# One fp32 product per head, two heads side by side in TensorE's rows, in place of three fp32r products of split operands

## The chip, the cores and the metric

The kernel runs on one core of one Trainium2 chip. The metric is the device time of one execution in microseconds, the median of three runs. The profile is of one execution of its own.

## The reference

Three layers follow one another: a linear recurrence over 768 steps for 4 batches of 8 heads of 48 channels, and two mixture layers (384 to 768 to 384 and 384 to 2048 to 384) on the 3072 tokens of 384 channels that it gives.

```python
for t in range(S):
    cur = np.einsum('bhd,bhe->bhde', u[None] * kt, vt)
    y[:, :, t] = np.einsum('bhd,bhde->bhe', rt, state + cur)
    state = wt[:, :, :, None] * state + np.einsum('bhd,bhe->bhde', kt, vt)
...
h = np.maximum(np.maximum(x @ w1, x @ w2), x @ w3)
return (h @ w_out).astype(np.float32)
...
h = x @ w_in
g = h - np.tanh(h)
return (g @ w_out).astype(np.float32)
```

## The kernel before, in words

**The recurrence** is done in 24 chunks of 128 steps, 6 to a batch; only the state goes from chunk to chunk. Partitions 0 to 47 and 64 to 111 hold the channels of the two heads of a pair, and the free axis the 4 pairs. For a chunk, `scans` takes running products of the decays w forwards (`fwd`) and backwards (`suf`) on VectorE, `decays` multiplies k by `suf` and r by `fwd` in place, `scores` makes k'r of every pair of steps on TensorE, `masked` copies the scores to `P` (ScalarE) and clears what lies in the future (GpSimd), `diagonal` writes the term with u (VectorE), `outputs` multiplies `P` by v and adds r times the state, and `outputs_out` copies the result out of PSUM and sends it by DMA into `xs`, the input of the first mixture layer. `key_turn` transposes k in 32 x 32 blocks on VectorE and sends the blocks through DRAM to their places, `key_order` copies them to `kcn`, and `state_mm`, `state_add` and `state_decay` carry the state on.

**Scores.** Chunks 0 to 4 (`c < EARLY`) multiply plain fp32: 8 products a chunk, each with 48 rows, head 0 in the array's rows 0 to 63 and head 1 in rows 64 to 127, into two banks (line 307). From chunk 5 on, `splits` (lines 284 to 292) first makes of k and of r a rounded fp32r part and the exact rest, r with zeros where the other head's rows are: per chunk three copies on ScalarE (287, 291 twice) and three subtractions on VectorE (288, 292 twice). `scores` then does three fp32r products (`mm3`, lines 491 to 493) of 128 x 256 for each pair, 12 a chunk, half of them in step `k0` and half in `k1`. From chunk 6 on `outputs_two` gives the output in two halves of two pairs, in steps `k3` and `k4`, into two banks: two products with the state of 112 columns (359), then four with v of 48 columns (362).

**The order of the work.** Chunks 0 to 3 come first (the prologue). Then six groups of 512 tokens go through the first mixture layer: 18 slots of 9 products with `WAh`, `WAl` (lines 491 to 493 on `xh`, `xl`), and after them 54 products with `WOh`, `WOl` (the O part). Beside the slots of group g the four chunks of group g+1 are worked on, five steps (`k0` to `k4`) each, spread over the slots; group 5 has none. Group 0 also converts weights from float64 (lines 64 to 73, 487, 488), 16 units of the 24. A scheduler puts the instructions of each engine into one fixed order, and each engine works its own through in that order. Line 683 splits the last part of the hidden layer (`hl`) of a group on VectorE; 410 and 411 split `xs` for the next group.

**Buffers.** `wt`, `rk` and `nt` hold a chunk's inputs. There are two of each, and a third (`third`) for chunk 2 alone, closed when the splits' pool opens; `load_next` loads two chunks ahead from chunk 3 on, all on SyncE's queue.

The banks in the rows are numbered from 85 on: `bank_89` to `bank_92` are `bank[4]` to `bank[7]`, that is the two score banks, `yab` and `dsb`; `rk_119` and `rk_120` are `rk[0]` and `rk[1]`, `P_127` and `P_128` the two `Pt`, `AS_130` and `AS_131` the two `ASt`.

Of the kernel before, what the change touches and what calls it, by code (L numbers as in the profile page):

```python
# [15 lines left out]
ALU = mybir.AluOpType  # L16
# [43 lines left out]

# float64 words (low, high) -> float32: sign and top exponent bit, 7 exponent bits and 23 of the mantissa;
# sizes below float32's are set to zero, those above to its largest
def abs_f64(act, raw, out):
# [26 lines left out]
def main_path(ctx, tc, wT, rkT, w0, rk0, nat, vpad, uT, ub, wA, wo1, wi2, wo2, outT, count):  # L90
# [11 lines left out]
    p_third = ExitStack()  # L102
    p_spl = ExitStack()
    wo1p = ctx.enter_context(pool_("wo1p"))
# [57 lines left out]

    Yb, spl = [], []

# [9 lines left out]
    def ring(c):  # L174
        return c if c < 3 else (c - 1) % 2

    def load_next(c):
        n = 3 if c == 0 else 4 if c == 1 else c + 2
        if c != 2 and n < NCH:
            load_att(n)  # L180

# [14 lines left out]

# [1 line left out]
    def aend():  # L198
# [53 lines left out]
    def key_turn(c):  # L252
        # blocks of 32 x 32 on the vector engine, the blocks' places through DRAM
        if needs_state(c):
            kb = fwd[:, 0:NP * C]
            dve.transpose(kb.rearrange("p (c a q) -> p c a q", c=4, q=32),
                          rk[ring(c)][:, 1].rearrange("p a (c q) -> p c a q", c=4))
            sp.dma_start(kbd[c % 2].rearrange("p a b q -> p (a b q)"), kb)
            src = kbd[c % 2].rearrange("(a i) c b q -> c i a (b q)", a=4)
            for q in range(4):  # L260
                sp.dma_start(kb[32 * q:32 * q + 32].rearrange("i (a x) -> i a x", a=4), src[q])
# [11 lines left out]

    # k a rounded part and the exact rest; r likewise, a head's columns zero in the other head's rows
    def splits_open():
        p_third.close()
        sp_ = p_spl.enter_context(pool_("spl"))
        spl.extend(sp_.tile([P, NP, C], F32R, name=f"k{x}") for x in "hl")
        spl.extend(sp_.tile([P, NP, 2, C], F32R, name=f"r{x}") for x in "hl")
        for t in spl[2:]:  # L280
            for j in range(2):
                act.mul(t[64 * j:64 * j + 64, :, 1 - j], ident[64 * j:64 * j + 64, None, :].to_broadcast([64, NP, C]), 0.0)

    def splits(c):
        r = rk[ring(c)]
        kh, kl, rh, rl = spl
        act.copy(kh, r[:, 1])
        dve.tensor_tensor(kl, r[:, 1], kh, ALU.subtract)
        for j in range(2):
            rows = slice(64 * j, 64 * j + 64)  # L290
            act.copy(rh[rows, :, j], r[rows, 0])
            dve.tensor_tensor(rl[rows, :, j], r[rows, 0], rh[rows, :, j], ALU.subtract)

    def scores(c, half, st):
        if c >= EARLY:
            st[half] = scb()
            kh, kl, rh, rl = spl
            for p in (2 * half, 2 * half + 1):
                mm3(st[half][:, p % 2 * 2 * C:(p % 2 + 1) * 2 * C], kh[:, p], kl[:, p],
                    rh[:, p].rearrange("p s t -> p (s t)"), rl[:, p].rearrange("p s t -> p (s t)"), True, True)  # L300
            return
        if half == 0:
            st["s"] = [scb(), scb()]
        for p in (2 * half, 2 * half + 1):
            for j in range(2):
                rows = slice(64 * j, 64 * j + HD)
                pe.matmul(st["s"][j][:, p * C:(p + 1) * C], rk[ring(c)][rows, 1, p, :], rk[ring(c)][rows, 0, p, :],
                          start=True, stop=True)

    def diagonal(c):  # L310
        for j, q in enumerate(probs(c)):
            d = sdt[c % 2][:, NP * j:NP * (j + 1), None] if c >= EARLY else sdt[c % 2][:, j::2, None]
            dve.copy_predicated(q, dmask[:, None, :].to_broadcast([P, NP, C]), d.to_broadcast([P, NP, C]))  # L313

# [4 lines left out]

    def masked(c, st, which=range(2)):  # L320
        for j in which:
            q = probs(c)[j]
            act.copy(q.rearrange("p a t -> p (a t)"), st[j] if c >= EARLY else st["s"][j])  # L323
            pool.affine_select(out=q, in_=q, compare_op=ALU.is_gt, fill=0.0, base=0,  # L324
                               pattern=[[0, NP], [1, C]], channel_multiplier=-1)
# [25 lines left out]

    def outputs_two(c, half, st):
        V, q = vals(c), probs(c)[half]
        first = c % NC_B == 0
        obk = (yab, st[1])
        to = slice(half * C, (half + 1) * C)
        if not first:
            for i in range(2):
                pe.matmul(obk[i][0:AC, to], ASt[c % 2][:, 2 * half + i], rk[ring(c)][:, 0, 2 * half + i], start=True, stop=False)  # L359
        for i in range(2):  # L360
            for j in range(2):
                pe.matmul(obk[i][64 * j:64 * j + HD, to], V[:, 2 * half + i, j], q[:, 2 * i + j], start=first, stop=True)  # L362

    def outputs(c, half, st=None):
        if c >= EARLY_B:
            return outputs_two(c, half, st)
        b = c % 2
        V = vals(c)
        Pc = probs(c)
        first = c % NC_B == 0  # L370
        for p in (2 * half, 2 * half + 1):
            if c < EARLY:
# [6 lines left out]
                pe.matmul(o, W[:, p, 0:2 * HD], Pc[0][:, p, :], start=False, stop=True)  # L379
                continue  # L380
            if not first:
                pe.matmul(yab[0:AC, p * C:(p + 1) * C], ASt[b][:, p], rk[ring(c)][:, 0, p, :], start=True, stop=False)
            for j in range(2):
                o = yab[64 * j:64 * j + HD, p * C:(p + 1) * C]
                h = 2 * p + j
                pe.matmul(o, nt[ring(c)][:, DM + h * HD:DM + (h + 1) * HD], ident, start=first, stop=False)
                pe.matmul(o, V[:, p, j], Pc[half][:, 2 * (p % 2) + j], start=False, stop=True)

    def outputs_out(c, col, st=None):
        if c < EARLY:  # L390
# [5 lines left out]
        y = yst[c % 2]  # L396
        if c >= EARLY_B:
            for i, o in enumerate((yab, st[1])):
                act.copy(y[0:AC, i::2], o[0:AC, 0:2 * C].rearrange("p (a t) -> p a t", a=2))
        else:  # L400
            act.copy(y[0:AC].rearrange("p a t -> p (a t)"), yab[0:AC])
        to = xs[:, :, col:col + C]
# [15 lines left out]
    def att_steps(c, col):  # L418
# [3 lines left out]
        def k0():  # L422
            scores(c, 0, st)
            if c >= EARLY:
                masked(c, st, [0])
            if n and n < EARLY_B:
                bonus(n)
            if n:
                scans(n)

        def k1():
            scores(c, 1, st)
            masked(c, st, [1] if c >= EARLY else [0, 1])
            if c < EARLY:
# [3 lines left out]
            if n:  # L438
                decays(n)
                if n == EARLY:  # L440
                    splits_open()
                if n >= EARLY:
                    splits(n)
                if n >= EARLY_B:
                    bonus(n)
                squares(n)
# [10 lines left out]
        def k3():  # L457
            outputs(c, 0, st)
            if n:
                bonus_sum(n)  # L460

        def k4():
            outputs(c, 1, st)
            outputs_out(c, col, st)
            if n and n < EARLY_B:
# [5 lines left out]
    def in_range():  # L471
        # every product of decays within 2^-60 .. 2^60: the chunk-wise form keeps float32's accuracy
        dve.tensor_scalar(sq, sq, 1.0, None, ALU.is_lt)
# [3 lines left out]

# [1 line left out]
    def w1_upto(n):  # L479
# [14 lines left out]

# [1 line left out]
    def pads(i):  # L496
# [6 lines left out]
    def warm(n):  # L503
        # columns for the array's activity monitor while it would rest
        for _ in range(n):
# [52 lines left out]
    for c in range(GROUPS[0]):  # L558
        st = {}
        n = c + 1  # L560
        scores(c, 0, st)
        scores(c, 1, st)
        key_turn_pe(c)
# [7 lines left out]
        state_decay(n)  # L571
        outputs(c, 0)
        outputs(c, 1)
        warm(WARM[3] if c < 2 else 0)
# [13 lines left out]

# [1 line left out]
    WO2 = W2a = None  # L590
# [43 lines left out]
    for g, gn in enumerate(GROUPS):  # L634
# [5 lines left out]
        if g == len(GROUPS) - 2:  # L640
            def w2_open():
                nonlocal W2a
                in_range()
                p_att.close()
                p_spl.close()
                yb = ctx.enter_context(pool_("yb", "right"))
# [59 lines left out]

# [1 line left out]
    hb = Ring([bank[0], bank[1]])  # L708
# [45 lines left out]

# [1 line left out]
@with_exitstack  # L756
# [115 lines left out]
def _layout(r, k, v, w, u, moe_w1, moe_w2, moe_w3, moe_w_out, moe2_w_in, moe2_w_out):  # L872
# [17 lines left out]

    # x: of tile k, rows 0..95 are the head pair k, rows 96..127 a third of the last pair
    row = np.arange(P)
# [51 lines left out]
```

## Time and profile before

| | |
|---|---|
| median of 3 runs | 907.84 us (907.41 to 911.14) |
| profiled execution, span | 906.0 us |
| TensorE busy (products) | 854.7 us, 94% |
| VectorE busy | 573.0 us, 63% |
| ScalarE busy | 373.0 us, 41% |
| GpSimd busy | 218.9 us, 24% |
| group 0 of the first layer | 55.4 to 133.6 us, its O part to 148.1 |
| group 5, without chunks beside it | 436.5 to 474.5 us |
| second layer alone | about 487 to 906 us |

The profile gives no time of its own around the span; the median lies 1.8 us above the span. Busy shares are means over stages with different limits, so the stages are read one by one. An fp32 product of the program shows as two records in the trace, an fp32r product as one.

### The profile page before, as it was taken

The page shows a single profiled execution, that of the slowest core. Times are in us where ns is not written, and L with a number is a line of the kernel's source. Part 1 is how long each engine was busy: PE and PEld are TensorE (multiplying, and loading weights), DVE is VectorE, ACT ScalarE, POOL GpSimd, SP SyncE. Part 2 cuts the span into 40 slices and gives each one's busy share as a digit, 9 for nine tenths or more (in the row PEclk, how much of TensorE's full clock was granted, in tenths as well). Part 3 has the DMA queues.
Part 4 walks back from the last instruction along what each step waited for, and adds up shares of the span by engine and source line. Part 5 has one row for each costly group of instructions (what it writes and reads, how often), then busy time and mean ns, then how long its engine had stood idle before and what let it go on. Part 6 is the DMA issues. An engine that isn't in the chain of part 4 may idle for free.

```text
span 906.0 us, 11870 instructions
## 1 busy us (share of the span) xinstructions
PE 854.7 (94%) x4342; PEld 678.0 (75%) x4342; DVE 573.0 (63%) x880; ACT 373.0 (41%) x736; POOL 218.9 (24%) x214
## 2 busy tenths in 40 slices
PE   7888789989989999999998999999999999999996
PEld 5767567868767877877886678888888888888884
DVE  8999998886766777785899944334334334333332
ACT  4655445445334454553446533223323224223232
POOL 6756443452433343351035300000000000000000
PEclk8989889999999999999999999999999999999999
DMA  8533533344134133332553300000000000000001
GB/s 258 174 123 97 172 85 102 109 118 130 54 104 131 48 116 114 102 108 68 156 152 106 87 1 6 31 0 22 14 1 35 1 1 35 0 1 35 1 0 39
DMA packets 40561, 66.47 MB, mean 73 GB/s; under 512 B 6256, under 2 KB 21360, under 8 KB 40496
## 3 DMA queue, kind: packets, MB, share of 16 engines
q1 hardware_dynamic: 40496, 65.64, 24.3%
q8 instruction: 36, 0.59, 0.3%
q14 instruction: 29, 0.24, 0.1%
HBM read 53.23 MB, written 8.65 MB: 68 GB/s over the span
## 4 chain that ended last, share of the span: by engine, by line
PE 55%; DVE 3%; DMA 1%; issue 1%; ACT 1%; POOL 0%; ACTq 0%; SPq 0%; DVEq 0%
PE bank L493 18%; PE bank L491 18%; PE bank L492 18%; DVE cv L73 1%; DVE cv L72 1%; DMA xs<-in_wi 0%; PE bank L362 0%; DMA xs<-in_wo 0%; DVE cv L71 0%; PE bank L359 0%; DVE hl L724 0%; DVE fwd L206 0%; DVE P L313 0%; DVE cv L70 0%; DVE rk L213 0%
## 5 line engine op out<-in xcount | busy, mean ns | idle before, releaser
L722 DVE TENSOR_TENSOR tmp<-bank,tmp 128x512 f32<-128x512 f32 x96 | 66.3, 691 | 174.8 <-ACT tmp L721 174.8
L491 PE MATMUL bank<-xh,WAh 128*128 128x512 f32 x324 | 136.2, 420 | 0.0
L721 ACT ACTIVATE tmp<-bank 128x512 f32<-128x512 f32 x96 | 57.4, 598 | 182.9 <-PE bank L493 182.9
L493 PE MATMUL bank<-xl,WAh 128*128 128x512 f32 x324 | 131.7, 406 | 0.0
L492 PE MATMUL bank<-xh,WAl 128*128 128x512 f32 x324 | 130.8, 404 | 0.0
L491 PE MATMUL bank<-hh,WO2h 128*128 128x512 f32 x288 | 114.1, 396 | 1.7 <-ACT hh L723 1.7
L493 PE MATMUL bank<-hl,WO2h 128*128 128x512 f32 x288 | 114.3, 397 | 0.7 <-DVE hl L724 0.7
L492 PE MATMUL bank<-hh,WO2l 128*128 128x512 f32 x288 | 113.7, 395 | 0.0
L724 DVE TENSOR_TENSOR hl<-tmp,hh 128x512 fp32r<-128x512 f32 x96 | 66.5, 692 | 59.1 <-PE bank L493 46.7
L723 ACT CAST hh<-tmp 128x512 fp32r<-128x512 f32 x96 | 59.5, 620 | 72.8 <-DVE tmp L722 72.7
L491 PEld LDWEIGHTS bank<-xh,WAh 128*128 128x128 f32 x324 | 62.5, 193 | 18.3 <-issue 5.8
L493 PEld LDWEIGHTS bank<-xl,WAh 128*128 128x128 f32 x324 | 62.6, 193 | 15.8 <-DVE xl L416 0.7
L492 PEld LDWEIGHTS bank<-xh,WAl 128*128 128x128 f32 x324 | 63.2, 195 | 11.9
L493 PEld LDWEIGHTS bank<-hl,WO2h 128*128 128x128 f32 x288 | 54.1, 188 | 16.0 <-DVE hl L724 3.3
L491 PEld LDWEIGHTS bank<-hh,WO2h 128*128 128x128 f32 x288 | 54.1, 188 | 15.6 <-ACT hh L723 3.2
L683 POOL TENSOR_TENSOR hl<-tmp,hh 128x512 fp32r<-128x512 f32 x30 | 44.1, 1471 | 87.3 <-ACT hh L682 87.2
L492 PEld LDWEIGHTS bank<-hh,WO2l 128*128 128x128 f32 x288 | 54.1, 188 | 12.8
L680 DVE TENSOR_TENSOR tmp<-bank,tmp 128x512 f32<-128x512 f32 x72 | 49.2, 684 | 15.1 <-PE bank L493 12.9
L313 DVE COPY_PREDICATED P<-dmask,sd 128x512 f32<-128x512 uint8 x36 | 35.7, 1011 | 25.2 <-POOL P L324 25.2
L324 POOL TENSOR_SCALAR_AFFINE_SELECT P<-P 128x512 f32<-128x512 f32 x44 | 33.2, 761 | 69.1 <-ACT P L323 69.0
L491 PE MATMUL bank<-xh,W2ha 128*128 128x512 f32 x108 | 43.5, 402 | 2.8 <-ACT Yb L704 2.8
L493 PE MATMUL bank<-hl,WOh 128*128 128x512 f32 x108 | 43.2, 402 | 2.9 <-DVE hl L683 1.6
(196 smaller groups left out, 1736.0 us busy)
## 6 DMA issues: line engine op xcount, KB each, us to landing
nt<-in_nat SPq DMA_DIRECT2D x19, 576.0 KB, 4.3
rk<-in_rkT SPq DMA_DIRECT2D x44, 192.0 KB, 3.3
Y<-in_wA SPq DMA_DIRECT2D x18, 384.0 KB, 5.5
w2st<-in_wi SPq DMA_DIRECT2D x12, 384.0 KB, 3.2
wt<-in_wT SPq DMA_DIRECT2D x44, 96.9 KB, 2.9
kbd<-fwd SPq DMA_DIRECT2D x15, 256.0 KB, 2.0
fwd<-kbd SPq DMA_DIRECT2D x60, 64.0 KB, 2.0
xs<-in_wo SPq DMA_DIRECT2D x8, 384.0 KB, 3.2
```

Of the source, the lines that this page charges most:

```text
L72: dve.scalar_tensor_tensor(oi, high, -0x40000000, oi, ALU.bitwise_and, ALU.bitwise_or)
L313: dve.copy_predicated(q, dmask[:, None, :].to_broadcast([P, NP, C]), d.to_broadcast([P, NP, C]))
L324: pool.affine_select(out=q, in_=q, compare_op=ALU.is_gt, fill=0.0, base=0, pattern=[[0, NP], [1, C]], channel_multiplier=-1)
L491: pe.matmul(bk, wh, ah, start=first, stop=False)
L492: pe.matmul(bk, wl, ah, start=False, stop=False)
L493: pe.matmul(bk, wh, al, start=False, stop=last)
L680: dve.tensor_tensor(t[:, 0:n], bk[:, 0:n], t[:, 0:n], ALU.max)
L683: (dve if f == F1 - 1 else pool).tensor_tensor(hl[:, f, 0:n], t[:, 0:n], hh[:, f, 0:n], ALU.subtract)
L721: act.activation(t, bk, AF.Tanh)
L722: dve.tensor_tensor(t, bk, t, ALU.subtract)
L723: act.copy(hh[:, r], t)
L724: dve.tensor_tensor(hl[:, r], t, hh[:, r], ALU.subtract)
```

## The change

All chunks take the plain fp32 scores of chunks 0 to 4, in one run in step `k0`, and `splits` with its pool goes. `outputs` runs once a chunk, in step `k4`, all four pairs into one bank; the product with the state is split into one of 48 columns for each head, so that the two heads of a pair stand in the two column halves in every term. The third buffer stays open and joins the ring, so inputs load three chunks ahead. Comments are taken out.

```diff
     def ring(c):
-        return c if c < 3 else (c - 1) % 2
+        return c % 3
     def load_next(c):
-        n = 3 if c == 0 else 4 if c == 1 else c + 2
-        if c != 2 and n < NCH:
-            load_att(n)
+        if c + 3 < NCH:
+            load_att(c + 3)
...
-    def splits_open():
...
-    def splits(c):
...
-    def outputs_two(c, half, st):
...
+    def scores(c, st):
+        st["s"] = [scb(), scb()]
+        for p in range(NP):
             for j in range(2):
                 rows = slice(64 * j, 64 * j + HD)
                 pe.matmul(st["s"][j][:, p * C:(p + 1) * C], rk[ring(c)][rows, 1, p, :], rk[ring(c)][rows, 0, p, :],
...
+    def outputs(c):
...
+            terms = []
             if not first:
-                pe.matmul(yab[0:AC, p * C:(p + 1) * C], ASt[b][:, p], rk[ring(c)][:, 0, p, :], start=True, stop=False)
+                terms.append(lambda j: (ASt[b][:, p, 64 * j:64 * j + HD], rk[ring(c)][:, 0, p, :]))
+            if c < EARLY_B:
+                terms.append(lambda j: (nt[ring(c)][:, DM + (2 * p + j) * HD:DM + (2 * p + j + 1) * HD], ident))
+            terms.append(lambda j: (V[:, p, j], Pc[j][:, p, :]))
+            for i, t in enumerate(terms):
+                for j in range(2):
+                    pe.matmul(yab[64 * j:64 * j + HD, p * C:(p + 1) * C], *t(j), start=i == 0, stop=i == len(terms) - 1)
...
         def k0():
-            scores(c, 0, st)
-            if c >= EARLY:
-                masked(c, st, [0])
+            scores(c, st)
+            masked(c, st)
...
         def k1():
-            scores(c, 1, st)
-            masked(c, st, [1] if c >= EARLY else [0, 1])
...
-                if n == EARLY:
-                    splits_open()
-                if n >= EARLY:
-                    splits(n)
...
         def k3():
-            outputs(c, 0, st)
             if n:
                 bonus_sum(n)
         def k4():
-            outputs(c, 1, st)
-            outputs_out(c, col, st)
+            outputs(c)
+            outputs_out(c, col)
```

In the rows that follow lines are those of each program: 491 to 493 before are 439 to 441 after, 307 is 278, 680 is 626, 683 is 629, 411 is 367, 313 is 283, 204 is 202 or 204 by its output, 212 and 213 are 210 and 211, 256 is 254.

TensorE, chunk 9's scores beside group 1's slots, before: six products, a slot of nine, six more.

```order
L491 MATMUL bank_89<-rh,kh 128x256
L492 MATMUL bank_89<-rh,kl 128x256
L493 MATMUL bank_89<-rl,kh 128x256
L491 MATMUL bank_89<-rh,kh 128x256
L492 MATMUL bank_89<-rh,kl 128x256
L493 MATMUL bank_89<-rl,kh 128x256
L491 MATMUL bank_87<-xh,WAh 128x512
```

The same place after, and the next product:

```order
L278 MATMUL bank_89<-rk_119 128x128
L278 MATMUL bank_90<-rk_119 128x128
L278 MATMUL bank_89<-rk_119 128x128
L278 MATMUL bank_90<-rk_119 128x128
L278 MATMUL bank_89<-rk_119 128x128
L278 MATMUL bank_90<-rk_119 128x128
L278 MATMUL bank_89<-rk_119 128x128
L278 MATMUL bank_90<-rk_119 128x128
L439 MATMUL bank_87<-xh,WAh 128x512
```

Twelve products in two places became eight in one, the banks of the two heads in turn.

VectorE at the end of group 0, before, from the last maximum of the hidden layer on:

```order
L680 TENSOR_TENSOR tmp_116<-bank_86,tmp_116 128x512
L205 RECIPROCAL d_126<-suf 128x4
L206 SCALAR_TENSOR_TENSOR fwd<-wt_118,d_126 128x516
L203 MEMSET d_126 128x5
L683 TENSOR_TENSOR hl<-tmp_116,hh 128x512
L212 TENSOR_TENSOR rk_120<-rk_120,suf 128x512
L213 TENSOR_TENSOR rk_120<-rk_120,fwd 128x512
L256 STREAM_TRANSPOSE fwd<-rk_120 128x512
L288 TENSOR_TENSOR kl<-rk_120,kh 128x512
L292 TENSOR_TENSOR rl<-rk_120,rh 64x4x128 x2
L232 TENSOR_REDUCE sd_135<-nt_122 128x8
L411 TENSOR_TENSOR xl<-xs,xh 128x512 x3
```

The same place after:

```order
L626 TENSOR_TENSOR tmp_116<-bank_86,tmp_116 128x512
L201 MEMSET d_126 128x5
L254 STREAM_TRANSPOSE fwd<-third 128x512
L629 TENSOR_TENSOR hl<-tmp_116,hh 128x512
L202 SCALAR_TENSOR_TENSOR suf<-wt_117,d_126 128x517
L203 RECIPROCAL d_126<-suf 128x4
L210 TENSOR_TENSOR rk_119<-rk_119,suf 128x512
L230 TENSOR_REDUCE sd_136<-nt_121 128x8
L367 TENSOR_TENSOR xl<-xs,xh 128x512
L283 COPY_PREDICATED P_127<-dmask,sd_135 128x512
L204 SCALAR_TENSOR_TENSOR fwd<-wt_117,d_126 128x516
L367 TENSOR_TENSOR xl<-xs,xh 128x512 x2
```

The scan of chunk 8 and its decays now stand ahead of `hl`, its three split operations are gone, and two of the three parts of `xl` stand behind a copy into `P` that needs chunk 8's scores and behind a scan of chunk 9.

## Rows read from the trace of the kernel before

**Rows 1.** Windows: us busy (instructions) of PE, PEld, DVE, ACT, POOL; clock, DMA.

```profile
55.40:133.60 78.20, 65.25 (x373) 50.25 (x372) 77.16 (x121) 39.77 (x86) 40.38 (x36) 0.89 0.36 111
...
148.10:208.20 60.10, 57.62 (x355) 45.50 (x353) 50.10 (x66) 26.86 (x58) 27.76 (x27) 0.97 0.38 112
...
221.10:281.10 60.00, 57.41 (x364) 44.77 (x362) 40.85 (x59) 25.43 (x54) 23.93 (x26) 0.97 0.32 92
281.10:295.80 14.70, 13.23 (x56) 10.10 (x55) 10.72 (x13) 6.97 (x15) 5.71 (x5) 1.00 0.42 125
...
351.90:366.20 14.30, 13.04 (x57) 10.20 (x55) 11.47 (x19) 7.30 (x17) 4.49 (x5) 1.00 0.48 140
...
436.50:474.50 38.00, 38.00 (x163) 30.52 (x163) 34.85 (x73) 18.35 (x36) 9.28 (x5) 1.00 0.50 143
```

**Rows 2.** Groups by form, TensorE, 148.1 to 423.7 us (groups 1 to 4).

```profile
L493 PE MATMUL bank<-rl,kh 128*128 128x256 f32 x64 | 18.9, 298 | 2.6 <-DVE rl L292 2.6
L491 PE MATMUL bank<-rh,kh 128*128 128x256 f32 x64 | 18.7, 292 | 1.9 <-ACT rh L291 1.6 <-ACT yst L399 0.2
L492 PE MATMUL bank<-rh,kl 128*128 128x256 f32 x64 | 18.6, 292 | 2.5 <-DVE kl L288 2.5
```

**Rows 3.** Timeline of TensorE in group 0: start, length, [idle before, what ended it].

```profile
118.57 0.58 PE L493 MATMUL bank<-rl,kh 128*128 128x256 f32 x1 [1.74 <-DVE rl L292]
```

**Rows 4.** Groups by form, VectorE, 55.4 to 133.6 us (group 0).

```profile
L292 DVE TENSOR_TENSOR rl<-rk,rh 64x512 fp32r<-64x512 f32 x6 | 6.0, 1008 | 0.1
L313 DVE COPY_PREDICATED P<-dmask,sd 128x512 f32<-128x512 uint8 x4 | 4.8, 1259 | 0.0
L206 DVE TENSOR_TENSOR_SCAN fwd<-wt,d 128x516 f32<-128x516 f32 x3 | 4.5, 1494 | 0.0
L212 DVE TENSOR_TENSOR rk<-rk,suf 128x512 f32<-128x512 f32 x3 | 3.9, 1284 | 0.0
...
L288 DVE TENSOR_TENSOR kl<-rk,kh 128x512 fp32r<-128x512 f32 x3 | 3.7, 1217 | 0.0
...
L213 DVE TENSOR_TENSOR rk<-rk,fwd 128x512 f32<-128x512 f32 x2 | 2.2, 1086 | 0.0
...
L256 DVE STREAM_TRANSPOSE fwd<-rk 128x512 f32<-128x512 f32 x2 | 1.4, 704 | 0.0
```

**Rows 5.** Line 288 over the whole span: ns least/median/most.

```profile
L288 DVE TENSOR_TENSOR kl<-rk,kh x19: 650/1110/1492, 75.7 to 403.0; 128x512 fp32r<-128x512 f32 x19
```

**Rows 6.** Timeline of TensorE in group 1: one half of a chunk's scores, and the next slot.

```profile
166.01 0.28 PE L491 MATMUL bank<-rh,kh 128*128 128x256 f32 x1
...
166.73 0.39 PE L491 MATMUL bank<-xh,WAh 128*128 128x512 f32 x1
```

**Rows 7.** Timeline of TensorE in the prologue: chunk 3's fp32 scores, and what follows.

```profile
40.81 1.18 PE L307 MATMUL bank<-rk 48*128 48x128 f32 x16
41.92 1.11 PE L271 MATMUL bank<-ident,rk 128*128 128x128 f32 x4
```

**Rows 8.** Timeline of TensorE in group 1: one half of a chunk's outputs, and the next slot.

```profile
203.80 0.60 PE L359 MATMUL bank<-rk,AS 128*112 128x128 f32 x4
204.33 0.64 PE L362 MATMUL bank<-P,nt 128*48 128x128 f32 x8
204.91 0.50 PE L491 MATMUL bank<-xh,WAh 128*128 128x512 f32 x1
205.24 0.40 PE L492 MATMUL bank<-xh,WAl 128*128 128x512 f32 x1
```

**Rows 9.** Timeline of TensorE, group 0's O part: the product that waits for `hl`.

```profile
139.36 0.51 PE L493 MATMUL bank<-hl,WOh 128*128 128x512 f32 x1 [1.29 <-DVE hl L683]
```

**Rows 10.** Windows of group 0 and the prologue, columns as in rows 1.

```profile
9.30:10.50 1.20, 1.09 (x16) 0.97 (x16) 1.17 (x2) 0.02 (x1) 1.20 (x2) 1.00 1.12 364
...
101.20:106.70 5.50, 5.00 (x25) 3.51 (x25) 5.50 (x7) 3.06 (x8) 3.98 (x4) 0.50 0.46 120
...
118.60:123.70 5.10, 5.10 (x15) 4.23 (x16) 5.10 (x10) 1.91 (x4) 1.72 (x2) 0.50 0.29 88
```

More of the change, by code (lines that the diff above doesn't have):

```diff
@@ L102, in main_path @@
     p_third = ExitStack()
-    p_spl = ExitStack()
     wo1p = ctx.enter_context(pool_("wo1p"))
@@ L161, in main_path @@
     kbd = [dramp.tile([P, 4, NP, 32], F32, name=f"kbd{i}") for i in range(2)]
-    Yb, spl = [], []
+    Yb = []
     def ys(d, g):
@@ L272, in key_turn_pe @@
             act.copy(kcn.rearrange("t b r -> t (b r)"), dsb)
-    def splits_open():
[L276 to L282, printed above, removed]
-    def splits(c):
[L285 to L294, printed above, removed]
-        if c >= EARLY:
[L296 to L304, printed above, removed]
+    def scores(c, st):
+        st["s"] = [scb(), scb()]
+        for p in range(NP):
             for j in range(2):
@@ L311, in diagonal @@
         for j, q in enumerate(probs(c)):
-            d = sdt[c % 2][:, NP * j:NP * (j + 1), None] if c >= EARLY else sdt[c % 2][:, j::2, None]
-            dve.copy_predicated(q, dmask[:, None, :].to_broadcast([P, NP, C]), d.to_broadcast([P, NP, C]))
+            dve.copy_predicated(q, dmask[:, None, :].to_broadcast([P, NP, C]),
+                                sdt[c % 2][:, j::2, None].to_broadcast([P, NP, C]))
     def bonus_vals(c):
@@ L318, in bonus_vals, with masked @@
             sdt[c % 2].rearrange("p (a s) -> p a s", s=2)[:, :, :, None].to_broadcast([P, NP, 2, HD]), ALU.mult)
-    def masked(c, st, which=range(2)):
-        for j in which:
+    def masked(c, st):
+        for j in range(2):
             q = probs(c)[j]
-            act.copy(q.rearrange("p a t -> p (a t)"), st[j] if c >= EARLY else st["s"][j])
+            act.copy(q.rearrange("p a t -> p (a t)"), st["s"][j])
             pool.affine_select(out=q, in_=q, compare_op=ALU.is_gt, fill=0.0, base=0,
@@ L350, in state_add @@
                     dve.tensor_tensor(S[rows], bv[rows], ASt[c % 2][rows, :, as_cols(c, 64 * j)], ALU.add)
-    def outputs_two(c, half, st):
[L353 to L366, printed above, removed]
+    def outputs(c):
         b = c % 2
@@ L370, in outputs @@
         first = c % NC_B == 0
-        for p in (2 * half, 2 * half + 1):
+        for p in range(NP):
             if c < EARLY:
@@ L380, in outputs, with outputs_out @@
                 continue
+            terms = []
             if not first:
-                pe.matmul(yab[0:AC, p * C:(p + 1) * C], ASt[b][:, p], rk[ring(c)][:, 0, p, :], start=True, stop=False)
[L383 to L389, printed above, removed]
+                terms.append(lambda j: (ASt[b][:, p, 64 * j:64 * j + HD], rk[ring(c)][:, 0, p, :]))
[3 more added lines that the diff above has]
+            for i, t in enumerate(terms):
+                for j in range(2):
+                    pe.matmul(yab[64 * j:64 * j + HD, p * C:(p + 1) * C], *t(j), start=i == 0, stop=i == len(terms) - 1)
+    def outputs_out(c, col):
         if c < EARLY:
@@ L396, in outputs_out @@
         y = yst[c % 2]
[L397 to L401, printed above, removed]
+        act.copy(y[0:AC].rearrange("p a t -> p (a t)"), yab[0:AC])
         to = xs[:, :, col:col + C]
@@ L422, in k0 @@
         def k0():
-            scores(c, 0, st)
-            if c >= EARLY:
-                masked(c, st, [0])
+            scores(c, st)
+            masked(c, st)
             if n and n < EARLY_B:
@@ L560, in main_path @@
         n = c + 1
-        scores(c, 0, st)
-        scores(c, 1, st)
+        scores(c, st)
         key_turn_pe(c)
@@ L571, in main_path @@
         state_decay(n)
-        outputs(c, 0)
-        outputs(c, 1)
+        outputs(c)
         warm(WARM[3] if c < 2 else 0)
@@ L644, in w2_open @@
                 p_att.close()
-                p_spl.close()
+                p_third.close()
                 yb = ctx.enter_context(pool_("yb", "right"))
```

## The prediction

> **What bounds the kernel now.** I read the windows by stage first. Group 5 has no chunk beside it and gives TensorE's own pace: 38.00 us for 162 products, 0.235 each, with no idle time [rows 1]. Every group with four chunks beside it has the same 162 products and takes longer: 60.1 and 60.0 us for groups 1 and 2, 78.2 for group 0. The excess, 22 us and 40 us, is the chunks' own products, waits and clock. So TensorE is the bound, but two things stretch its time in the groups. In group 0 VectorE is busy 77.16 of 78.20 us [rows 1]: it converts weights and works on the chunks, and TensorE waits for it. In groups 1 and 2 TensorE has gaps, and its granted clock is 0.97 of full in the mean: 6% of the group at 1.2 instead of 2.4 GHz, which costs 3% of it.
>
> Then I asked who ends the gaps. In groups 1 to 4 the first product of each kind of the split scores waited 2.6 us for the rests of r, 2.5 for the rest of k and 1.6 for the rounded r, 6.7 us in all [rows 2]. In group 0 one such wait alone is 1.74 us [rows 3]. The clock falls behind these waits and stays down: the 5.1 us after that wait ran at 0.50 [rows 10].
>
> What is after group 5 (from 487 us) contains nothing of the recurrence; the change shifts it as a whole, and I give it no gain.
>
> **The change, part by part.**
>
> *VectorE in group 0.* Up to the subtraction that makes the group's last `hl`, the order holds nine split operations: 6 of 1008 ns and 3 of 1217 ns, 6.0 + 3.7 = 9.7 us [rows 4]. All go. In the new order, chunk 8's decays and its transpose stand ahead of that `hl`; before, they stood behind it. That adds 1.28 + 1.09 + 0.70 = 3.1 us [rows 4], besides a short reduction that I leave out. If the nine are worth what they took, `hl` comes 6.6 us earlier. But the same shape took 650 ns at least and 1492 at most [rows 5]: part of the nine's time is waiting inside the instruction, and GpSimd is busy 40 of the 78 us beside it [rows 1]. At 0.65 each the nine are worth 5.9 us, and the gain is 2.8. I take the middle, **-4.7 us**, since nothing says which of the next VectorE operations inherits the blocked time. TensorE's own savings in group 0 count nothing more: VectorE sets the pace there.
>
> The Trainium skill, page "SBUF — State Buffer", section "Who interferes with whom", says that a VectorE instruction with two SBUF inputs contends with a GpSimd instruction that reads SBUF, and that the loser waits for the whole of the other's instruction. By that rule the blocked time belongs to GpSimd's work, which stays: the gain here is 2.8 us and the time 887.3. If the nine's whole time went, it would be 883.5. The spread of 650 to 1492 ns in one shape agrees with the rule; no row shows where the time goes once the nine are out.
>
> *Waits and clock in groups 1 to 4.* The 6.7 us of [rows 2] go with their cause: scores now wait only for `decays`, which the splits also waited for. The clock loss in groups 1 and 2 is 3% of 120.1 us = 3.6 us [rows 1], and it goes if the idle stretches before it go. **-10.3 us.**
>
> *A new wait.* At the start of group 1, VectorE's order now has a copy into `P` (chunk 8) and a scan ahead of two of the three parts of `xl`. The copy needs the scores that TensorE does just there, through ScalarE and GpSimd. The two take 1.26 + 1.49 = 2.75 us [rows 4] behind that path; TensorE has eleven products between (2.6 us by its pace) and the state's eight small ones. Bounds: 0 if the path is covered, 4 us if it takes as long again as the copy. I take **+1.5 us**. In groups 2 to 4 the order puts `xl` ahead of that copy.
>
> *TensorE's work, 16 chunks (8 to 23).* Scores now: half a chunk is 166.73 - 166.01 = 0.72 us [rows 6], 1.44 a chunk. The eight fp32 products of chunk 3 took 41.92 - 40.81 = 1.11 us to the next instruction [rows 7]. Sixteen records in that time is 0.069 each, while the fp32 records with 112 columns follow at 0.43 / 4 = 0.108 (0.53 us less a switch, [rows 8]): two heads do run side by side. Changing between full array and halves costs: the product after the outputs came 0.33 us before the next instead of 0.235, 0.10 us [rows 8]. The 1.11 holds one switch; with entry and the late product it is 1.31. Gain 0.13 a chunk, 2.1 us in 16.
>
> Outputs now: from 203.80 to 205.24 less one product at pace, 1.44 - 0.235 = 1.21 us a half [rows 8], 2.41 a chunk. After: eight column pairs in one run. A pair took 0.24 (0.58 less a switch, halved), an undivided product 0.215 [rows 8]; 8 x 0.22 to 0.24 and three times 0.10 make 2.06 to 2.22. Gain 0.19 to 0.36, I take 0.3: 4.8 us in 16. The split of the state's product thus costs nothing, since its two halves share the time of one. Together **-6.9 us**, between -5.1 and -7.8.
>
> *O parts.* In the O parts of groups 2 and 3 TensorE was idle 14.70 - 13.23 = 1.5 and 14.30 - 13.04 = 1.3 us [rows 1]; in group 0's, 1.29 us for `hl` [rows 9], already in the first term. `hl` now has no scan between it and its maximum. **-2.0 us**, between 0 and -2.8.
>
> *At nothing:* ScalarE loses three copies a chunk; it is busy 40 of 78 us in group 0 [rows 1], so nobody waits for it in the mean. The loads move one chunk earlier on SyncE's queue; DMA is at 0.32 to 0.38 of its engines' time in groups 0 to 2 [rows 1], and the queue waits for the same readers, a chunk's outputs. If that cover failed, the scans would wait, which they can do now as well. Scores and both masks in one step instead of two move work forward only.
>
> **Sum:** -4.7 - 10.3 + 1.5 - 6.9 - 2.0 = -22.4. The profiled span of 906.0 becomes 883.6; the median lies 1.8 above that execution, so **885.4 us**.
>
> **The rivals.**
>
> *A. The waits form again.* VectorE's order is fixed; each step also waits for TensorE's banks, so freed time can turn into another wait (for `kcn` through DRAM, for `P`). Then only TensorE's work (-6.9), the least of group 0 (-2.8) and the new wait (+1.5) count: -8.2, 899.6 us. For it: three hops per chunk remain. Against: after group 0 VectorE is busy 50 and 41 of 60 us [rows 1] and loses over 2 us a chunk of it.
>
> *B. The halves don't overlap here.* Then eight products at 0.215 and three switches make 2.02 us a chunk instead of 1.31: 0.71 x 16 = 11.4 us, 896.8. Against: [rows 7]. The page "FP8 and Floating Point Precision" of the Trainium skill, section "TensorE Precision Notes", has true fp32 at four passes through the array; the trace agrees (0.215 for 128 columns, 0.235 for 512 of fp32r), and this is what would make the change cost time without the overlap.
>
> *C. Slower: the clock.* Runs of half-filled array could count as rest, and the clock fall behind each. A stretch of 5.3 us at 0.50, as the two in [rows 10], costs 2.65 us. With one in each of 16 chunks that is 42 us: 928 us. It decides from about nine stretches on (22.4 / 2.65). Against: the fp32 scores at 9.3 to 10.5 us ran at 1.00 [rows 10], and both low stretches followed idle time.
>
> *D. More goes than I counted.* Group 0 loses the full 9.7 us, its wait for `hl` (1.3) and the two low stretches in it (10.6 / 2 = 5.3); the rest at its best (10.3, 7.8, 2.8): -37.2, 870.6 us.
>
> **The numbers.** Forecast 0.66, A 0.15, D 0.12, C 0.04, B 0.03. By its terms' bounds the forecast runs from 880 (-27.5) to 894 (-14.2), or 897 if the clock gives nothing back. The range 869 to 897 takes in most of D and B; it leaves out C and most of A, under 2 in 10. A measurement tells some 0.5%, 4.5 us, from no change. Only A's upper end is within it, and C alone is slower: faster 0.91, same 0.05, slower 0.04.
>
> **What would show it.** Group 0 ends near 129 us and its O part near 143; groups 1 and 2 take some 54 to 56 us, at a clock of 1.00; group 1 opens with a short gap ended by `xl`; a chunk's scores span about 1.1 us and its outputs about 2. I am wrong if TensorE's idle time in groups 1 to 4 stays above 8 us under new names, if group 0 does not end earlier, or if low clock follows fp32 runs.

## The result, and the profile after

The changed kernel takes 882.01 us (median of 4 runs, 881.04 to 882.85), the kernel before, run beside it, 907.62 (4 runs, 906.34 to 911.14). The ratio is 0.9712, with a 95% interval from 0.9692 to 0.9733. The forecast was 885.4 us, with a range of 869 to 897. The profiled execution spans 880.7 us, 25.3 less than that of before.

The windows of the kernel after, by stage, have the columns of [rows 1]:

```profile
55.20:94.50 39.30, 38.99 (x249) 30.64 (x248) 34.56 (x59) 17.01 (x38) 21.02 (x21) 0.92 0.30 89
94.50:107.40 12.90, 0.39 (x2) 0.00 (x0) 12.43 (x20) 6.46 (x13) 7.20 (x7) 0.68 0.32 76
107.40:131.10 23.70, 21.94 (x141) 17.05 (x141) 18.77 (x32) 9.86 (x21) 10.79 (x10) 0.88 0.58 182
131.10:147.10 16.00, 14.27 (x74) 10.57 (x73) 12.68 (x20) 6.05 (x13) 6.28 (x6) 1.00 0.20 56
147.10:202.40 55.30, 54.49 (x402) 41.70 (x401) 40.44 (x59) 20.41 (x44) 26.64 (x27) 1.00 0.44 125
...
215.10:268.30 53.20, 53.20 (x404) 41.03 (x402) 31.18 (x49) 19.08 (x40) 22.74 (x27) 1.00 0.36 104
268.30:281.10 12.80, 12.80 (x56) 10.18 (x55) 7.64 (x13) 5.91 (x12) 2.63 (x2) 1.00 0.53 156
```

The first three rows are group 0, the fourth its O part; then come groups 1 and 2, and group 2's O part. The table puts the stages side by side (A is a group's first layer, O its second; from the first product of each stage):

| us | before | after | difference |
|---|---|---|---|
| start of group 0 | 55.4 | 55.2 | -0.2 |
| group 0, A and O | 78.2 + 14.5 | 75.9 + 16.0 | -0.9 |
| groups 1 to 4, A | 233.7 | 214.5 | -19.2 |
| groups 1 to 4, O | 54.7 | 51.0 | -3.7 |
| from group 5 on | 469.5 | 468.1 | -1.4 |

So nearly all of it came from groups 1 to 4, where TensorE now has hardly a break (54.49 of 55.30 us busy in group 1, 53.20 of 53.20 in group 2, clock 1.00 in both). Group 0, which the prediction credited with 4.7 us, gave almost nothing.

The groups by form of TensorE in groups 1 to 4 show what is left in place of [rows 2]; besides this wait for `xl` there is one of 0.2 for `kcn`:

```profile
L441 PE MATMUL bank<-xl,WAh 128*128 128x512 f32 x216 | 85.7, 398 | 0.8 <-DVE xl L367 0.8
...
L278 PE MATMUL bank<-rk 48*128 48x128 f32 x160 | 11.6, 285 | 0.0
```

A chunk's outputs and scores in group 1 (timeline of TensorE, as [rows 6, 8]):

```profile
159.21 0.40 PE L441 MATMUL bank<-xl,WAh 128*128 128x512 f32 x1
159.54 0.43 PE L347 MATMUL bank<-third,AS 128*48 128x128 f32 x4
...
161.42 0.50 PE L439 MATMUL bank<-xh,WAh 128*128 128x512 f32 x1
161.76 0.40 PE L440 MATMUL bank<-xh,WAl 128*128 128x512 f32 x1
...
163.40 0.40 PE L441 MATMUL bank<-xl,WAh 128*128 128x512 f32 x1
163.73 1.16 PE L278 MATMUL bank<-rk 48*128 48x128 f32 x16
164.82 0.50 PE L439 MATMUL bank<-xh,WAh 128*128 128x512 f32 x1
165.15 0.39 PE L440 MATMUL bank<-xh,WAl 128*128 128x512 f32 x1
```

The full-array product ahead of each of them and the one behind it take 0.33 to 0.34 us to the next start instead of 0.235. With both delays, the outputs take 161.76 - 159.21 - 2 x 0.235 = 2.08 us (before 2.41) and the scores 165.15 - 163.40 - 2 x 0.235 = 1.28 (before 1.44). Before, the products ahead of these places kept the pace of 0.235.

Group 0 has one long stop. The timelines of SyncE, ScalarE and TensorE there:

```profile
79.20 0.33 SPq L256 DMA_DIRECT2D kbd<-fwd  x1
...
81.53 1.76 SPq L259 DMA_DIRECT2D fwd<-kbd  x4
```
```profile
97.15 0.51 ACT L435 CAST WAh<-cv 128x384 fp32r<-128x384 f32 x1
...
100.78 0.51 ACT L435 CAST WAh<-cv 128x384 fp32r<-128x384 f32 x1 [1.75 <-DVE cv L73]
...
103.41 0.51 ACT L435 CAST WAh<-cv 128x384 fp32r<-128x384 f32 x1 [1.19 <-DVE cv L73]
103.83 1.07 ACT L294 COPY P<-bank 128x512 f32<-128x512 f32 x2
106.34 0.51 ACT L435 CAST WOh<-cv 128x384 fp32r<-128x384 f32 x1 [1.45 <-DVE cv L73]
106.76 0.62 ACT L263 COPY kcn<-fwd 128x512 f32<-128x512 f32 x1
```
```profile
107.43 0.88 PE L311 MATMUL bank<-nt,kcn 128*48 128x48 f32 x16 [12.54 <-ACT kcn L263]
```

Chunk 6's keys were sent back from DRAM from 81.53 us on, but `kcn` was copied only at 106.76, because in ScalarE's order the copy stands behind casts of weight units, and three of the four shown waited for VectorE's conversion. TensorE's next product in its order needed `kcn`, and TensorE stood from 94.89 on. Before, the same wait was 3.28 us long (SyncE, ScalarE, TensorE):

```profile
92.84 1.75 SPq L261 DMA_DIRECT2D fwd<-kbd  x4
```
```profile
100.48 0.65 ACT L265 COPY kcn<-fwd 128x512 f32<-128x512 f32 x1
```
```profile
101.18 0.88 PE L340 MATMUL bank<-nt,kcn 128*48 128x48 f32 x16 [3.28 <-ACT kcn L265]
```

### The profile page after: what moved, and what is told of

Same layout as the page of the kernel before. It is cut to its first block, busy times and chain, and to the rows that moved or that the text cites. A ratio compares the mean times of both kernels' runs of the same rounds, so it can differ in the third digit from the quotient of the medians.

```text
span 880.7 us, 12116 instructions
## 1 busy us (share of the span) xinstructions
PE 839.4 (95%) x4546; PEld 663.7 (75%) x4546; DVE 514.6 (58%) x823; ACT 335.8 (38%) x657; POOL 211.3 (24%) x214
## 4 chain that ended last, share of the span: by engine, by line
PE 82%; DVE 10%; DMA 2%; issue 2%; POOL 1%; SPq 1%; ACT 1%; DVEq 0%; ACTq 0%; POOLq 0%
PE bank L439 26%; PE bank L441 25%; PE bank L440 25%; PE bank L347 3%; DVE cv L72 2%; PE bank L278 2%; DVE cv L73 2%; DMA Y<-in_wA 1%; DVE cv L71 1%; PE bank L311 1%; DVE cv L70 1%; DVE fwd L204 1%; DVE suf L202 0%; DMA rk<-in_rkT 0%; DVE hl L670 0%
## 5 line engine op out<-in xcount | busy, mean ns | idle before, releaser
L669 ACT CAST hh<-tmp 128x512 fp32r<-128x512 f32 x96 | 59.7, 621 | 72.8 <-DVE tmp L668 72.7
L629 POOL TENSOR_TENSOR hl<-tmp,hh 128x512 fp32r<-128x512 f32 x30 | 46.5, 1550 | 106.5 <-ACT hh L628 106.5
L626 DVE TENSOR_TENSOR tmp<-bank,tmp 128x512 f32<-128x512 f32 x72 | 49.0, 680 | 18.6 <-PE bank L441 14.5
L283 DVE COPY_PREDICATED P<-dmask,sd 128x512 f32<-128x512 uint8 x36 | 32.8, 950 | 45.6 <-POOL P L295 45.6
L628 ACT CAST hh<-tmp 128x512 fp32r<-128x512 f32 x36 | 22.4, 621 | 88.2 <-DVE tmp L626 85.3
L439 PE MATMUL bank<-hh,WOh 128*128 128x512 f32 x108 | 43.3, 401 | 0.4 <-ACT hh L628 0.4
```

Source lines behind the costliest of these rows:

```text
L439: pe.matmul(bk, wh, ah, start=first, stop=False)
L626: dve.tensor_tensor(t[:, 0:n], bk[:, 0:n], t[:, 0:n], ALU.max)
L628: act.copy(hh[:, f, 0:n], t[:, 0:n])
L629: (dve if f == F1 - 1 else pool).tensor_tensor(hl[:, f, 0:n], t[:, 0:n], hh[:, f, 0:n], ALU.subtract)
L669: act.copy(hh[:, r], t)
```

## The experiments

The theory after this profile: in groups 1 to 4 the waits for the splits and some of TensorE's work are gone; in group 0 the gain was lost to ScalarE's order. Rivals: the outputs' part is the main one; VectorE's time, not the waiting for the splits, is what counted; group 0 is bound by VectorE whatever the order. "A" and "O" below are sums over groups 1 to 4 of the profiled execution.

**The outputs' part alone**, on the kernel before:

```diff
-        if c >= EARLY_B:
-            return outputs_two(c, half, st)
+        if c >= EARLY_B:
+            return outputs_one(c) if half else None
...
```

> The second part alone: the splits and the fp32r scores stay, only the outputs of chunks 8 to 23 go in one run of column halves. Theory: 0.3 us in each of 16 chunks at most, and part of it is lost in the waits for the splits that stay: 903 to 906 us; the waits for rh, kl and rl in groups 1 to 4 stay near 6 us. Rival (outputs are the main part): 895 us or less.

Measured 903.77 us, ratio 0.9978 (0.9955 to 1.0); the profiled span is 900.9. A 228.4 (5.3 less than before), O 55.4. The waits for `rh`, `kl` and `rl` stay, 7.8 us in all, in other shares, and one for `kcn` grows (groups by form, groups 1 to 4):

```profile
L489 PE MATMUL bank<-rl,kh 128*128 128x256 f32 x64 | 18.6, 296 | 5.7 <-DVE rl L292 5.7
...
L340 PE MATMUL bank<-nt,kcn 128*48 128x48 f32 x208 | 7.3, 212 | 3.4 <-ACT kcn L265 3.4
```

**The scores' part alone**, first with a wide state product ahead of each pair of column halves:

```diff
-                terms.append(lambda j: (ASt[b][:, p, 64 * j:64 * j + HD], rk[ring(c)][:, 0, p, :]))
+                pe.matmul(yab[0:AC, p * C:(p + 1) * C], ASt[b][:, p], rk[ring(c)][:, 0, p, :], start=True, stop=False)
...
```

> The change without its second part: all scores in plain fp32, heads side by side, no splits, three buffers; but the outputs of chunks 8 to 23 in two halves, with the state's product over 112 columns, as before. Theory (the scores' part takes away the waits, the outputs' part only 0.3 us of TensorE's work in each of 16 chunks): groups 1 to 4 stay without waits at clock 1.00, each about 1.2 us longer than with the whole change, about 887 us (885 to 889). Rival (the outputs in one run are what smooths the chunks): 895 us or more, with new waits in groups 1 to 4.

Measured 898.41 us, ratio 0.9914 (0.988 to 0.9947), which is the rival's number but not its reason: TensorE waited only 0.6 us for `xl` and 0.2 for `kcn` in groups 1 to 4. The timeline shows a half of the outputs that takes 245.37 - 243.95 = 1.42 us, where the same six products took 1.11 in [rows 8]:

```profile
243.95 0.38 PE L341 MATMUL bank<-rk,AS 128*112 128x128 f32 x2
244.26 0.42 PE L347 MATMUL bank<-P,nt 128*48 128x128 f32 x4
244.61 0.47 PE L341 MATMUL bank<-rk,AS 128*112 128x128 f32 x2
245.01 0.43 PE L347 MATMUL bank<-P,nt 128*48 128x128 f32 x4
245.37 0.50 PE L440 MATMUL bank<-xh,WAh 128*128 128x512 f32 x1
```

The order differs: wide, pair, wide, pair instead of two wide and two pairs. With it come two more changes of shape and 0.31 us, 0.16 for each. The bank differs too: all six go into one bank instead of two, each pair right behind the wide product that it adds to. How much of the 0.16 is the shape and how much the bank was not separated. So this run was no clean "scores alone", and I ran it again in the order of the kernel before:

```diff
+            for i, p in enumerate(which):
+                if not first:
+                    pe.matmul(obk[i][0:AC, to], ASt[b][:, p], rk[ring(c)][:, 0, p, :], start=True, stop=False)
+            for i, p in enumerate(which):
+                for j in range(2):
+                    pe.matmul(obk[i][64 * j:64 * j + HD, to], V[:, p, j], Pc[j][:, p, :], start=first, stop=True)
...
```

> The scores' part alone again, now with the outputs of chunks 8 to 23 exactly in the order of the kernel before: in each half first the two state products over 112 columns, in two banks, then the four column halves (the run before this one alternated a wide product with a pair, and each change of shape showed some 0.1 us). Theory: a half takes 1.10 us as in the kernel before, two halves with their entries and exits some 0.4 us more than one run of 1.88; 16 chunks: 887 to 890 us, so that the scores' part brings about 19 us and the outputs' part the rest. Rival (cutting the outputs in two costs 16 us in whatever order): 896 us or more.

Measured 890.34 us, ratio 0.9805 (0.977 to 0.984), just past the upper end of what was expected, far from the rival. A is 220.7, O 50.9. From before to this kernel A loses 13.0 us and O 3.8; from this kernel to the whole change A loses another 6.2. A half of the outputs reads as before:

```profile
239.93 0.60 PE L333 MATMUL bank<-rk,AS 128*112 128x128 f32 x4
240.46 0.64 PE L336 MATMUL bank<-P,nt 128*48 128x128 f32 x8
241.03 0.51 PE L454 MATMUL bank<-xh,WAh 128*128 128x512 f32 x1
```

**Side by side or not:**

```diff
-        for p in range(NP):
-            for j in range(2):
+        for j in range(2):
+            for p in range(NP):
```

> The change with the four score products of head 0 ahead of the four of head 1, so that neighbours use the same row half. Theory (two row halves work side by side only where neighbours alternate: a pair-step is 0.112 us, a product alone 0.215): a chunk's scores take 0.6 to 0.8 us longer; 16 chunks beside a TensorE that is the bound make 10 to 13 us: 892 to 895 us. Rival (the order of the eight doesn't matter, or the scores are hidden): 881 to 884 us.

Measured 891.84 us, ratio 0.9844 (0.9811 to 0.9878). The scores now take 165.78 - 164.14 = 1.64 us instead of 1.09:

```profile
164.14 1.71 PE L278 MATMUL bank<-rk 48*128 48x128 f32 x16
165.78 0.50 PE L439 MATMUL bank<-xh,WAh 128*128 128x512 f32 x1
```

That is 0.55 us in each of 16 chunks, 8.8; A grew by 7.8 us, to 222.3. The overlap is real and rests on the order of neighbours; it is worth a little less than expected (891.84 us, with 892 to 895 expected).

**Two buffers instead of three:**

```diff
-        return c % 3
+        return c if c < 3 else (c - 1) % 2
...
```

> The change with two buffers for a chunk's inputs and the loads at the places of the kernel before, instead of three. Theory (nobody waited for a load before, and nobody does now): 881 to 884 us. Rival (the earlier loads carry part of the gain): scans or decays wait for loads, 887 us or more.

Measured 880.91 us, ratio 0.9697 (0.9665 to 0.9729). A 213.8, O 51.3: the third buffer and the earlier loads carry none of the gain. In group 0 the long stop is not there: the two longest waits for `kcn` are 3.62 and 3.96 us, and group 0 with its O part takes 89.2 us instead of 91.9, at a granted clock of 0.86 instead of 0.89. The stop of 12.54 us thus belongs to the order that the scheduler made with three buffers.

**The splits as work that nobody reads**, on the kernel with two buffers:

```diff
+                if n == EARLY:
+                    splits_open()
+                if n >= EARLY:
+                    splits(n)
...
```

> The change with two buffers, and with the splits of r and k made as before on VectorE and ScalarE from chunk 5 on, though nothing reads them: work added, the result unchanged. Theory (in groups 1 to 4 the cost of the splits was that the scores waited for them, not VectorE's time): group 0 ends 4 to 8 us later, groups 1 to 4 keep their length within 1 us each and show no new waits: 885 to 891 us. Rival (VectorE's time is what counted): groups 1 to 4 grow by 2 us or more each, 895 us or more.

Measured 907.08 us, ratio 1.0011 (0.9989 to 1.0033): my theory falls. A is 226.8 and O 58.5, 13.0 and 7.2 more than without the splits, although the scores don't read them. The waits stand in groups 1 to 4 under other names (groups by form of this kernel), and with three of them the granted clock fell again (0.91 in group 1's O part, 0.97 in groups 2 and 4, where it is 1.00 without the splits):

```profile
L464 PE MATMUL bank<-hh,WOh 128*128 128x512 f32 x55 | 22.9, 416 | 3.2 <-ACT hh L653 3.2
L466 PE MATMUL bank<-hl,WOh 128*128 128x512 f32 x55 | 22.5, 409 | 2.1 <-DVE d L203 2.1
L332 PE MATMUL bank<-nt,kcn 128*48 128x48 f32 x208 | 8.0, 223 | 10.1 <-ACT kcn L265 10.1
```

How a split makes `kcn` late is seen in group 2, in the timelines of VectorE, SyncE and TensorE:

```profile
262.76 1.44 DVE L288 TENSOR_TENSOR kl<-rk,kh 128x512 fp32r<-128x512 f32 x1
264.12 2.52 DVE L292 TENSOR_TENSOR rl<-rk,rh 64x512 fp32r<-64x512 f32 x2
266.65 0.71 DVE L256 STREAM_TRANSPOSE fwd<-rk 128x512 f32<-128x512 f32 x1
```
```profile
267.39 0.34 SPq L258 DMA_DIRECT2D kbd<-fwd  x1
267.83 0.65 SPq L380 DMA_DIRECT2D xs<-yst  x1
...
270.52 1.95 SPq L261 DMA_DIRECT2D fwd<-kbd  x4
```
```profile
274.76 0.88 PE L332 MATMUL bank<-nt,kcn 128*48 128x48 f32 x16 [3.42 <-ACT kcn L265]
```

The splits hold the transpose for 3.9 us. Its two transfers then stand on SyncE's queue, the second behind four stores of the outputs, and TensorE comes to the state's product before `kcn` is there.

**The same unread work, behind the transpose.** In the run above the splits stood ahead of the transpose in 11 of the 15 chunks that have both (not in half of them, as the expectation below says); here in two, chunk 14 and in part chunk 20, and neither had a wait for `kcn`:

```diff
         def k3():
             if n:
                 bonus_sum(n)
+                if n >= EARLY:
+                    splits(n)
...
```

> As the run before with splits that nobody reads, but VectorE makes them behind the turn of the chunk's keys (its transpose) in every chunk; in that run half of the transposes stood behind the splits and the waits in groups 1 to 4 were for kcn. Same work added, result unchanged. Theory (what the splits cost in groups 1 to 4 is their place: 3.9 us of VectorE ahead of the transpose, which makes the keys' way through DRAM late): the waits for kcn there shrink below 3 us in all, groups 1 to 4 lose 8 to 13 us, 893 to 898 us. Rival (VectorE's time as such, wherever it stands): within 4 us of the run before, 903 to 910 us.

Measured 897.41 us, ratio 0.9902 (0.9874 to 0.993). The time is where the theory put it, the waits are not: A 221.4 and O 57.2, 5.4 and 1.3 less than in the run before, and `kcn` still costs 6.2 us:

```profile
L464 PE MATMUL bank<-hh,WOh 128*128 128x512 f32 x55 | 22.9, 417 | 3.1 <-ACT hh L653 3.1
...
L332 PE MATMUL bank<-nt,kcn 128*48 128x48 f32 x208 | 7.7, 218 | 6.2 <-ACT kcn L265 6.2
```

So by these profiles the place of the splits is worth 6.7 of the 20.2 us that unread splits cost in groups 1 to 4. The other 13.5 are again waits, `kcn` and `hh` above all, and low clock that came with two of them (0.90 in group 1's O part, 0.97 in group 3). That this part would stay at any place is an argument, since only two places were run: the work fills VectorE and ScalarE, and the next copies and casts in their fixed orders come later. Which of the two engines' shares weighs more was not separated.

**Group 0, keys first.** The copy into `kcn` of chunk 6 goes ahead of the casts of units 15 and later, by an order without a wait:

```diff
-        act.copy(hi, g)
+        cast = act.copy(hi, g)
+        if behind is not None:
+            tc.add_manual_dep(cast.ins, behind.ins.name, mybir.DependencyInfo(
+                mybir.DependencyClass.NoSync, mybir.DependencyReason.DATA), reason="kcn first")
...
```

> The change, with one order altered in group 0: ScalarE makes chunk 6's kcn ahead of the casts of weight units 15 to 18 (before, behind them). Theory (group 0 gained little because TensorE stood still for 12.9 us, from 94.5 to 107.4, for this kcn, whose data had long been there, while the copy stood behind casts that wait for VectorE): the stretch shrinks to 3 us or less, and the group ends earlier by what VectorE's later idle time lets go, some 5 us (3 to 9): 877 us (873 to 879). Rival (VectorE's conversions set group 0's end whatever the order): the wait only moves to later products, 880.5 to 882.5 us.

Measured 879.01 us, ratio 0.97 (0.9668 to 0.9732). Group 0 with its O part takes 86.9 us instead of 91.9. The stop is 6.45 us long instead of 12.54; what held `kcn` now is a cast of `hh`, which waits for a maximum on VectorE, with the copies into `P` behind it (TensorE, then ScalarE):

```profile
99.70 0.88 PE L311 MATMUL bank<-nt,kcn 128*48 128x48 f32 x16 [6.45 <-ACT kcn L263]
```
```profile
95.26 0.62 ACT L633 CAST hh<-tmp 128x512 fp32r<-128x512 f32 x1 [3.64 <-DVE tmp L631]
...
98.07 1.06 ACT L294 COPY P<-bank 128x512 f32<-128x512 f32 x2
99.01 0.64 ACT L263 COPY kcn<-fwd 128x512 f32<-128x512 f32 x1
```

A second wait, ahead of chunk 7's products with `P`, grew from 1.73 to 3.45 us.

**Keys ahead of these too:**

```diff
-    kc, after_kcn = {}, {u: 6 for u in range(15, 24)}
+    kc, after_kcn = {}, {u: 6 for u in range(13, 24)}
...
+                    if g == 0 and slot == 8:
+                        hold(r, 6)
...
```

> The change, with chunk 6's kcn on ScalarE ahead also of a cast of hh that waits for VectorE, of the copies into P and of weight units 13 and 14. Theory (the rest of that wait, 6.8 us, is still ScalarE's order): it shrinks below 1 us; VectorE was idle 4.4 of the 71 us of group 0, so 2 to 5 us go: 874 to 877 us. Rival (VectorE's own work is now the bound of group 0): 878 to 880 us, the wait stands at another product.

Measured 884.07 us, ratio 0.9732 (0.97 to 0.9764), slower than both theories said. The wait for `kcn` is gone, and another, longer than the 6.45 us of keys first, stands behind it, at chunk 6's outputs:

```profile
109.43 1.93 PE L349 MATMUL bank<-P,nt 128*48 128x128 f32 x12 [8.54 <-DVE P L283]
```

VectorE reaches the copy into `P` only behind conversions, scans and maxima. Group 0 with its O part took 88.7 us. This execution also entered group 0 at 57.9 us, 2.7 later than the change's, ahead of anything that was edited.

**Chunks 6 and 7**, with the edit of keys first:

```diff
...
+    kc, after_kcn = {}, {**{u: 6 for u in range(15, 19)}, **{u: 7 for u in range(19, 24)}}
```

> The change (three buffers) with chunk 6's kcn ahead of the casts of units 15 to 18, as in the run with keys first, and chunk 7's kcn ahead of units 19 to 23. Theory: group 0 with its O part again some 4 us shorter than in the change's two profiles (91.9 and 90.4 us), and chunk 7's wait of 0.7 to 1.4 us goes: 877 to 880 us. Rival (the 879.0 us of keys first was the chip of that call): 881 to 884 us.

Measured 880.39 us, ratio 0.97 (0.9684 to 0.9715); group 0 with its O part 88.8. Between theory and rival: chunk 7's wait for `kcn` is gone, but the one ahead of its products with `P` is 4.24 us long (1.73 in the change), so the order of chunk 7 added nothing.

**Two buffers with keys first, and the change again beside it:**

```diff
...
+    kc, after_kcn = {}, {**{u: 6 for u in range(17, 21)}, **{u: 7 for u in range(21, 24)}}
```

> The change with two buffers and, in group 0, kcn of chunk 6 on ScalarE ahead of the casts of weight units 17 to 20, kcn of chunk 7 ahead of units 21 to 23. Theory (with two buffers group 0 still has two waits of 4.0 and 4.4 us for kcn, whose data had landed 5 us before; the first goes whole, the second stays in part behind a cast of hh): VectorE's idle time there, 4.5 us, is the most that can go, 2 to 4 us, 876 to 879 us. Rival (VectorE is the bound): 880 to 882 us.

> The change itself once more, beside the two kernels of this call, so that differences of a few us are read on one chip. Every theory expects 881 to 883 us; if it comes out at 879 or less, the gains of the two orders with keys first are not larger than the spread between chips.

Measured 881.4 us, ratio 0.9726 (0.97 to 0.9751), and 883.81 us, ratio 0.9764 (0.9738 to 0.979), for the change itself. With two buffers the wait for chunk 6's `kcn` shrank from 3.62 to 1.41 us, that for chunk 7's stayed (3.96 and 4.24), and one of 3.97 for `P` came up:

```profile
110.01 0.42 PE L348 MATMUL bank<-P,nt 128*48 128x128 f32 x2 [3.97 <-DVE P L284]
```

Group 0 took 89.5 us with its O part, where two buffers alone took 89.2: the rival's case. The change itself measured 882.01 and 883.81 at two times, with 91.9 and 90.4 us for group 0. Keys first (879.01) is the fastest median of all, and its group 0 is 3.5 to 5.0 us shorter; but its interval overlaps that of the change's first measurement, and the two were never measured side by side. That it beats the change is likely, not shown.

## Why the prediction was right, and where it was not

The sign, the range and the size (25.6 us against 22.4) held. That the size held is in part luck: in the profile (25.3) group 0 gave 3.8 us less than its term, and everything else 6.7 more. Of the signs that it named, the lengths of groups 1 and 2 (55.3 and 53.2 us), their clock, the gap for `xl` and the spans of scores and outputs came out; the ends of group 0 and its O part (129 and 143) did not: they are 131.1 and 147.1. By its steps:

- *VectorE in group 0, -4.7: the step that failed.* Group 0 with its O part lost 0.9 us. VectorE did get its time back: it is busy 34.56 + 12.43 + 18.77 = 65.8 of 75.9 us instead of 77.16 of 78.2 [rows 1]. But the step took VectorE's freed time for TensorE's, on the ground that VectorE sets the pace. In the changed kernel the pace was set by a chain through three orders: conversions on VectorE, casts on ScalarE, and `kcn` behind them. Chunk 6's keys were sent back from DRAM 11.3 us earlier than before (81.53 instead of 92.84), yet their copy came 6.3 us later (106.76 instead of 100.48), and TensorE was ready for it 3.0 us earlier; so the wait grew from 3.28 to 12.54 us. Keys first gave 3.5 to 5.0 us of it back, about what the step had promised; further moves found the next wait (`P`, 8.54 us). This is rival A's mechanism, in group 0 alone. The loads, which the prediction put at nothing, seem to have a part in it: with two buffers group 0 and its O part took 89.2 us, 3.5 less than before. These are single profiles, and the change's own two differ by 1.5.
- The rule on the shared port that I weighed there: conversions in L72 became dearer once the splits were out. Over group 0 and its O part, the 17 of L72 took 750 ns each before and 858 after, 12.5 and 14.6 us:

```profile
L72 DVE SCALAR_TENSOR_TENSOR cv<-Y,cv 128x384 int32<-128x384 int32 x17 | 14.6, 858 | 0.2
```

  The Trainium skill, page "SBUF — State Buffer", section "Who interferes with whom", says that a VectorE instruction with two SBUF inputs contends with a GpSimd instruction that reads SBUF. L72 would agree, if the blocked time of the splits passed to it; L73, of the same shape, doesn't: it fell from 11.5 to 10.6. The four lines of the conversions (L70 to L73) together took 41.7 us instead of 39.1. That the port is the cause was not tried.
- *Waits and clock in groups 1 to 4, -10.3, with the new wait +1.5:* net -8.8, somewhat too small. A lost 19.2; less TensorE's work as measured below, about 11 remain. Read directly, TensorE's idle time in A fell from 8.1 to 1.0 us, and the low clock of groups 1 and 2 (3.6) went. The clock is at 1.00 in all four groups, and the new wait at the start of group 1 is there, 0.8 us for `xl`. The reason was too narrow: I wrote that the scores no longer wait for the splits. Unread splits, however, cost 20.2 us in A and O together. They delay whatever comes after them, and when the scores don't wait, the state's product does.
- *TensorE's work, -6.9: right.* Scores gave 0.16 us a chunk, with 0.13 forecast, and outputs 0.33, with 0.3: 0.49 x 16 = 7.8, the edge of the bounds. The pair of runs with and without the outputs' part differs by 6.2 in A, waits included.
- *O parts, -2.0:* -3.7 in groups 1 to 4. Those of groups 1 and 4 had no idle time before either; those of groups 2 and 3 lost 1.9 and 1.6 us, more than the idle time that was read, since a product after a wait is late itself (0.34 us to the next start instead of 0.235 behind [rows 9]).
- *From group 5 on, nothing:* -1.4 us. Over all profiles, of whichever kernel, this stretch takes 468.1 to 469.5 us, so this is their spread and no gain of the change.
- *The rivals:* B is refuted by the run with the heads in turn, C by the clock of 1.00 in groups 1 to 4. Of these stages only group 0 shows less: 0.92 ahead of its stop, 0.68 in it and 0.88 after it. The low clock of the first row began at 51.4 us, near the end of 3.39 us of idle time, the other within the stop. D did not come, since group 0 did not follow.

## What to carry to other kernels

Work taken off an engine that is busy all the time is worth its time only if the chain that TensorE waits for gets shorter; follow that chain through each engine's fixed order before crediting it, since here the place of one copy (`kcn`) in ScalarE's order kept TensorE waiting for 12.5 us, and moving it gave 3.5 to 5.0 of them back. To find out whether readers wait for a piece of work or whether its time counts, run it unread, and once more at another place in the order. And keep products of one array shape together, or try it both ways: the outputs that alternated shapes, within one bank, cost 8.1 us more, a third of what the change had brought.

## What the runs showed of the hardware

- Between a full-array product and products of 48 rows or 48 columns, the product ahead of the change and the one behind it each took 0.33 to 0.34 us to the next start instead of 0.235.
- Outputs that alternate between products of 112 columns and column halves, in one bank, took 1.42 us for the six products that took 1.11 in two blocks and two banks: 0.16 for each further change. The kernel with them was 8.1 us slower (898.41 against 890.34).
- Two fp32 products in different row halves run side by side as neighbours in the order: 1.09 us for a chunk's eight, and 1.64 with all four of one head ahead of the other's.
- The start of group 0 lay between 55.2 and 57.9 us over the profiles, 55.2 and 56.1 for the same kernel. Single profiles of this kernel thus differ by about 1 us before the first stage; why was not tried.
